# Two-matmul SiLU kernel: the fourth 128-row piece of x and the first columns of w1 change places on one DMA queue, and the first column tiles are cut 384 + 128 rows instead of 256 + 256

## The chip, the cores and the metric

One core of a Trainium2 chip runs the kernel. The time is device microseconds for one launch, as the median of the runs; the profile is one further execution, whose span runs from its first to its last profiled instruction. Engines in the profile: PE is TensorE (matmuls), PEld its weight loads, DVE is VectorE, ACT is ScalarE, POOL is GpSimd, SP is SyncE, which here only issues DMAs. ACT issues some DMAs too ("ACTq").

## The reference

All three inputs are bf16: `x` is 1 x 2048 x 640, `w1` is 640 x 1728, `w2` is 1728 x 640.

```
h   = einsum("bsd,df->bsf", x, w1)      # 2048 x 1728
h   = silu(h)                           # h * sigmoid(h)
out = einsum("bsf,fd->bsd", h, w2)      # 2048 x 640
```

## The kernel before

The kernel is written as a plan: `add(engine, emit, deps)` appends one operation, and `build` emits each engine's operations in the order in which they were added, with a semaphore wait ahead of an operation for each dependency. Nothing is reordered afterwards, so the order of the `add` calls is the order of every engine's queue. An engine that waits holds up all that was added for it later.

The rows of x (2048) are worked in four chunks of 512 rows (`sc` = 0 to 3). The first matmul needs x transposed (`xT_sb`: 128 of the 640 inputs on the partitions, in five groups `dt`, and the rows along the free dimension). Chunks 1 to 3 are transposed by DMA (L230). Chunk 0 would come too late that way: it is loaded plainly in four 128-row pieces j = 0 to 3 (`load_x0`, L144, 160 KB each), and PE transposes each piece in five 128 x 128 steps (L166) into two PSUM banks, 2j and 2j+1. DVE copies three of the five results to `xT_sb` (L172), ACT the other two (L174).

`w1` comes in four DMAs (`load_w1`, L149) of 256, 256, 512 and 704 columns; `w1_0` is the first one, the columns of output tiles `ft` = 0 and 1 (320 KB). Before the change, ACT issues piece 1, piece 3 and then `w1_0`; SP issues pieces 0 and 2 and, when piece 2 has landed, the other three parts of w1, then the transposing DMAs and w2.

While the first loads are under way PE runs six matmuls on constants (L157, five of 512 columns and one of 256), whose results are not used. Then come the 20 transposes, and then the first matmul in units. `unit(sc, ft, c0, n)` is one output tile of 128 columns of w1 by n rows of x: five matmuls that accumulate over `dt` in one PSUM bank (L208), then `silu`: ACT writes the sigmoid to SBUF (L192) and DVE multiplies it with the PSUM tile into `hT_sb` (L195). Unit after unit takes the next of eight banks. A unit of chunk 0 waits for the copies of the last piece that its rows touch, and for its part of w1:

```
def x_deps(sc, c0, n):
    return xT_ready[(c0 + n) // P - 1] if sc == 0 else [x_dma[sc]]
```

The tiles `ft` = 0 and 1 of chunk 0 are cut along the rows at `XE`, which is 256 before the change: two units on rows 0 to 255 (pieces 0 and 1), then two on rows 256 to 511. Every later unit has 512 rows. After 13 full tiles for each chunk and the 64-column tail of w1 (L218), the second matmul (L282) runs to the end, with 64-row weight tiles in pairs; DVE (L294) and ACT (L297) move its results out of PSUM, and SP stores them.

Of the kernel before, what the change touches and what calls it, by code (L numbers as in the profile page):

```python
# [20 lines left out]
class Plan:  # L21
# [9 lines left out]
    def add(self, eng, emit, deps=(), group=None):  # L31
        op = Op(eng, emit, [d for d in deps if d is not None], group)
        self.ops.append(op)
        return op
# [40 lines left out]
def bass_standalone__dense_activation_silu__prompt_kernel(  # L75
# [13 lines left out]
    P = 128  # L89
    H = P // 2  # L90
    SCH = 512
# [6 lines left out]
    JB = SCH // P  # L98
# [4 lines left out]
    with ExitStack() as es:  # L103
        def sb(name, shape, dtype):
            return es.enter_context(nc.sbuf_tensor(name, shape, dtype))
# [8 lines left out]
        x0_sb = sb("x0_sb", [P, JB, D], bf16)  # L114
        ident = sb("ident", [P, P], bf16)
# [9 lines left out]
        bank_free = [[] for _ in range(NBANK)]  # L125
        turn = [0]

        def take_bank():
            b = turn[0] % NBANK
            turn[0] += 1  # L130
            return b


        XE = 2 * P
        w1_cuts = [0, 2, 4, 8, FT]
        id_a = add("pool", lambda e: e.memset(ident[:, :], 0.0))  # L136
        id_b = add("pool", lambda e: e.affine_select(  # L137
            out=ident[:, :], in_=ident[:, :], compare_op=ALU.not_equal, fill=1.0,
            base=0, pattern=[[-1, P]], channel_multiplier=1), [id_a])
# [3 lines left out]
        def load_x0(eng, j):  # L143
            return add(eng, lambda e: e.dma_start(  # L144
                out=x0_sb[:, j, :], in_=x0_v[:, j, :]), group=f"x0_{j}")

        def load_w1(eng, g, deps=()):
            f0, f1 = w1_cuts[g] * P, min(w1_cuts[g + 1] * P, F)
            return add(eng, lambda e: e.dma_start(  # L149
                out=w1_sb[:, :, f0:f1], in_=w1_v[:, :, f0:f1]), deps, group=f"w1_{g}")  # L150

        x0_of = [load_x0(eng, j) for j, eng in enumerate(("sp", "act", "sp", "act"))]
        w1_dma = [load_w1("act", 0)] + [load_w1("sp", g, [x0_of[2]]) for g in (1, 2, 3)]

        ones = nc.const_aps.tensor(1.0, [P, SCH], bf16)
        for n in [SCH] * 5 + [2 * P]:
# [1 line left out]
                ps[:, NBANK - 1, 0:n], lhsT=ones[:, 0:P], rhs=ones[:, 0:n], start=True, stop=True))  # L158

        xT_ready = []  # L160
        for j in range(JB):
            cols = slice(j * P, (j + 1) * P)
            ready = []
            for b, d0, d1, eng in ((2 * j, 0, TPV, "dve"), (2 * j + 1, TPV, DT, "act")):
                for dt in range(d0, d1):
                    t = add("pe", lambda e, j=j, b=b, dt=dt, d0=d0: e.transpose(  # L166
                        ps[:, b, :].bitcast(bf16)[:, (dt - d0) * P:(dt - d0 + 1) * P],
                        x0_sb[:, j, dt * P:(dt + 1) * P], ident[:, :]), [x0_of[j], id_b])
                src = ps[:, b, :].bitcast(bf16)[:, 0:(d1 - d0) * P].rearrange("p (k s) -> p k s", s=P)
                dst = xT_sb[:, d0:d1, cols]  # L170
                if eng == "dve":
                    c = add("dve", lambda e, src=src, dst=dst: e.tensor_copy(out=dst, in_=src), [t])  # L172
                else:
                    c = add("act", lambda e, src=src, dst=dst: e.copy(out=dst, in_=src), [t])  # L174
                ready += [c] * (d1 - d0)
                bank_free[b] = [c]
            xT_ready.append(ready)

        def x_deps(sc, c0, n):
            return xT_ready[(c0 + n) // P - 1] if sc == 0 else [x_dma[sc]]  # L180

        def w1_deps(ft):
            return [w1_dma[max(g for g in range(len(w1_dma)) if w1_cuts[g] <= ft)]]
# [5 lines left out]
        def silu(b, parts, n, pe):  # L189
            s = sig_turn[0] % NSIG  # L190
            sig_turn[0] += 1
            a = add("act", lambda e: e.activation(  # L192
                out=sig_sb[:, s, 0:n], in_=ps[:, b, 0:n], func=ACT.Sigmoid), [pe, sig_free[s]])
            for rows, ft, cols in parts:
                v = add("dve", lambda e, rows=rows, ft=ft, cols=cols: e.tensor_tensor(  # L195
                    out=hT_sb[rows, ft, cols], in0=ps[rows, b, 0:n], in1=sig_sb[rows, s, 0:n],
                    op=ALU.mult), [a])
                chunk_done[cols.start // SCH] = v
                if ft == FR:
                    tail_done[cols.start // SCH] = v  # L200
            bank_free[b] = [v]
            sig_free[s] = v

        def unit(sc, ft, c0, n):
            b = take_bank()
            cols = slice(sc * SCH + c0, sc * SCH + c0 + n)
            for dt in range(DT):
                pe = add("pe", lambda e, dt=dt: e.matmul(  # L208
                    ps[:, b, 0:n], lhsT=w1_sb[:, dt, ft * P:(ft + 1) * P], rhs=xT_sb[:, dt, cols],
                    start=(dt == 0), stop=(dt == DT - 1)),  # L210
                    x_deps(sc, c0, n) + w1_deps(ft) + bank_free[b] if dt == 0 else ())
            silu(b, [(slice(0, P), ft, cols)], n, pe)
# [27 lines left out]
                    w2_dma.append(add("sp", lambda e, hh=hh: e.dma_start(  # L240
                        out=w2_sb[hh * H:(hh + 1) * H, FR, :], in_=w2[FR * P:F, :]), group="w2"))

        for c0 in (0, XE):
            for ft in range(2):
                unit(0, ft, c0, XE)
        for ft in range(2, FR):
            unit(0, ft, 0, SCH)

# [18 lines left out]
        for pi, (sa, sbt) in enumerate(pairs):  # L267
# [3 lines left out]
            for q in range(4):  # L271
                h = q % 2
                c0, c1 = (LAST_SPLIT if pi == len(pairs) - 1 else SPLIT)[h:h + 2]
# [5 lines left out]
                for ft in range(n_ft):  # L279
                    for t, rows in ((lo_t, slice(0, H)), (hi_t, slice(H, P))):  # L280
                        b = banks[t, h]
# [9 lines left out]
                for k, t in enumerate((sa, sbt)):  # L291
                    b = banks[t, h]
# [45 lines left out]
```

## Time and profile before

| | |
|---|---|
| median of 3 runs | 127.2 us (127.02, 127.20, 129.05) |
| the profiled execution, its own time | 127.36 us |
| its span | 125.9 us |
| PE busy | 122.1 us (97% of the span) |
| DVE busy | 48.4 us (38%) |
| ACT busy | 42.4 us (34%) |
| first matmul of the first unit (L208) starts at | 6.03 us |

The profiled execution's time is 1.5 us more than its span: that lies before the first and after the last profiled instruction. "Busy" for PE counts overlapping matmuls once, and a matmul's record is longer than the spacing of matmuls in a stream, as they are pipelined; where a cost per matmul is needed, the spacing of the starts is used. In a timeline line the first number is the start in the span, the second the length, and the bracket holds the idle time before it on that engine and what ended it. A merged line ("x45") covers several instructions in a row.

### The profile page before, as it was taken

The page shows a single profiled execution, that of the slowest core. Times are in us where ns is not written, and L with a number is a line of the kernel's source. Part 1 is how long each engine was busy: PE and PEld are TensorE (multiplying, and loading weights), DVE is VectorE, ACT ScalarE, POOL GpSimd, SP SyncE. Part 2 cuts the span into 40 slices and gives each one's busy share as a digit, 9 for nine tenths or more (in the row PEclk, how much of TensorE's full clock was granted, in tenths as well). Part 3 has the DMA queues.
Part 4 walks back from the last instruction along what each step waited for, and adds up shares of the span by engine and source line. Part 5 has one row for each costly group of instructions (what it writes and reads, how often), then busy time and mean ns, then how long its engine had stood idle before and what let it go on. Part 6 is the DMA issues. An engine that isn't in the chain of part 4 may idle for free.

```text
span 125.9 us, 2647 instructions
## 1 busy us (share of the span) xinstructions
PE 122.1 (97%) x1175; PEld 72.0 (57%) x1180; DVE 48.4 (38%) x79; ACT 42.4 (34%) x78; POOL 0.7 (1%) x6
## 2 busy tenths in 40 slices
PE   7899999999999999999999999999999999999993
PEld 2774444444444444444457777777777777777662
DVE  0454666666666666666673111103011110301103
ACT  4445555555555555555540111102011110201102
POOL 2000000000000000000000000000000000000000
PEclk9999999999999999999999999999999999999999
DMA  4898743599900000000000030200202020020303
GB/s 122 232 346 262 117 84 86 94 346 386 191 7 0 5 0 3 0 0 0 0 5 0 0 109 0 79 31 0 104 5 104 0 85 24 5 104 0 109 0 104
DMA packets 15819, 9.92 MB, mean 79 GB/s; under 512 B 8896, under 2 KB 15808, under 8 KB 15808
## 3 DMA queue, kind: packets, MB, share of 16 engines
q1 hardware_dynamic: 14576, 8.93, 24.5%
q10 hardware_dynamic: 1232, 0.82, 2.1%
q8 instruction: 9, 0.15, 0.5%
q14 instruction: 2, 0.02, 0.0%
HBM read 5.16 MB, written 2.62 MB: 62 GB/s over the span
## 4 chain that ended last, share of the span: by engine, by line
PE 97%; issue 0%; ACT 0%; DVE 0%
PE ps L282 47%; PE ps L208 45%; PE ps L157 2%; PE ps L218 2%; PE ps L166 2%; ACT xT_sb L174 0%; DVE o_sb L294 0%
## 5 line engine op out<-in xcount | busy, mean ns | idle before, releaser
L282 PE MATMUL ps<-w_sb,hT_sb 64*128 64x320 bf16 (+2 forms) x864 | 58.9, 296 | 0.0
L208 PE MATMUL ps<-xT_sb,w_sb 128*128 128x512 bf16 (+1 forms) x265 | 56.3, 373 | 0.8 <-ACT xT_sb L174 0.5
L282 PEld LDWEIGHTS ps<-w_sb,hT_sb 64*128 64x128 bf16 x864 | 41.7, 94 | 17.4 <-issue 0.4
L195 DVE TENSOR_TENSOR hT_sb<-ps,sig_sb 128x512 bf16<-128x512 f32 (+2 forms) x58 | 39.1, 673 | 22.6 <-ACT sig_sb L192 22.2
L208 PEld LDWEIGHTS ps<-xT_sb,w_sb 128*128 128x128 bf16 x270 | 26.5, 98 | 30.4 <-DVE xT_sb L172 0.8
L192 ACT ACTIVATE sig_sb<-ps 128x512 bf16<-128x512 f32 (+1 forms) x56 | 32.6, 582 | 27.1 <-PE ps L208 26.0
L294 DVE CAST o_sb<-ps 128x320 bf16<-128x320 f32 (+2 forms) x16 | 7.9, 491 | 48.9 <-PE ps L282 48.9
L297 ACT CAST o_sb<-ps 128x320 bf16<-128x320 f32 (+2 forms) x16 | 6.8, 425 | 51.7 <-PE ps L282 51.7
L157 PE MATMUL ps<-const-bfloat16-1.0 128*128 128x512 bf16 (+1 forms) x6 | 2.5, 588 | 0.8 <-PEq L323 0.8
L172 DVE COPY xT_sb<-ps 128x384 bf16<-128x384 bf16 x4 | 1.4, 358 | 3.4 <-PE ps L166 3.4
L166 PEld LDWEIGHTS ps<-ident,x_sb 128*128 128x128 bf16 x20 | 2.1, 147 | 0.6 <-DMA x_sb<-in_x_dram 0.6
L218 PE MATMUL ps<-xT_sb,w_sb 128*64 128x512 bf16 x20 | 2.4, 382 | 0.0
L166 PE MATMUL ps<-ident,x_sb 128*128 128x128 bf16 x20 | 2.3, 313 | 0.0
L174 ACT COPY xT_sb<-ps 128x256 bf16<-128x256 bf16 x4 | 1.5, 372 | 2.2 <-PE ps L166 2.2
L157 PEld LDWEIGHTS ps<-const-bfloat16-1.0 128*128 128x128 bf16 x6 | 0.7, 133 | 1.9 <-issue 1.9
L218 PEld LDWEIGHTS ps<-xT_sb,w_sb 128*64 128x64 bf16 x20 | 1.1, 110 | 1.2 <-issue 0.4
L141 ACT ACT_TABLE_LOAD x1 | 1.3, 1283 | 0.7 <-PEq L323 0.7
L140 DVE MEMSET warm_sb<- 128x32 f32 x1 | 0.1, 85 | 0.8 <-PEq L323 0.8
L137 POOL TENSOR_SCALAR_AFFINE_SELECT ident<-ident 128x128 bf16<-128x128 bf16 x1 | 0.3, 292 | 0.2 <-POOL ident L136 0.2
L141 ACT ACTIVATE warm_sb<-warm_sb 128x32 f32<-128x32 f32 x1 | 0.2, 229 | 0.0
L136 POOL MEMSET ident<- 128x128 bf16 x1 | 0.2, 204 | 0.3 <-POOLq L323 0.3
L323 POOL MEMSET const-bfloat16-1.0<- 128x1 bf16 x1 | 0.1, 101 | 0.0
(3 smaller groups left out, 0.3 us busy)
## 6 DMA issues: line engine op xcount, KB each, us to landing
out_dram<-o_sb SPq DMA_DIRECT2D x14, 160.0 KB, 1.9
w_sb<-in_w_dram SPq DMA_DIRECT2D x1, 1120.0 KB, 7.6
w_sb<-in_w_dram SPq DMA_DIRECT2D x1, 960.0 KB, 5.4
w_sb<-in_w_dram SPq DMA_DIRECT2D x1, 880.0 KB, 7.0
w_sb<-in_w_dram SPq DMA_DIRECT2D x1, 640.0 KB, 5.3
x_sb<-in_x_dram SPq DMA_DIRECT2D x2, 160.0 KB, 2.6
x_sb<-in_x_dram ACTq DMA_DIRECT2D x2, 160.0 KB, 2.8
w_sb<-in_w_dram ACTq DMA_DIRECT2D x1, 320.0 KB, 4.1
```

The source lines that it names most:

```text
L141: add("act", lambda e: e.activation(out=warm_sb[:, :], in_=warm_sb[:, :], func=ACT.Sigmoid), [warm])
L157: add("pe", lambda e, n=n: e.matmul(ps[:, NBANK - 1, 0:n], lhsT=ones[:, 0:P], rhs=ones[:, 0:n], start=True, stop=True))
L166: t = add("pe", lambda e, j=j, b=b, dt=dt, d0=d0: e.transpose(ps[:, b, :].bitcast(bf16)[:, (dt - d0) * P:(dt - d0 + 1) * P], x0_sb[:, j, d ...
L172: c = add("dve", lambda e, src=src, dst=dst: e.tensor_copy(out=dst, in_=src), [t])
L174: c = add("act", lambda e, src=src, dst=dst: e.copy(out=dst, in_=src), [t])
L192: a = add("act", lambda e: e.activation(out=sig_sb[:, s, 0:n], in_=ps[:, b, 0:n], func=ACT.Sigmoid), [pe, sig_free[s]])
L195: v = add("dve", lambda e, rows=rows, ft=ft, cols=cols: e.tensor_tensor(out=hT_sb[rows, ft, cols], in0=ps[rows, b, 0:n], in1=sig_sb[rows, ...
L208: pe = add("pe", lambda e, dt=dt: e.matmul(ps[:, b, 0:n], lhsT=w1_sb[:, dt, ft * P:(ft + 1) * P], rhs=xT_sb[:, dt, cols], start=(dt == 0), ...
L218: pe = add("pe", lambda e, dt=dt, hh=hh: e.matmul(ps[hh * H:(hh + 1) * H, b, :], lhsT=w1_sb[:, dt, FR * P:F], rhs=xT_sb[:, dt, (sc + hh) * ...
L282: last[t] = add("pe", lambda e, t=t, rows=rows, b=b, n=n, ft=ft, q=q, cols=cols: e.matmul(ps[:, b, 0:n], lhsT=hT_sb[rows, ft, t * P:(t + 1 ...
L294: ev = add("dve", lambda e, t=t, b=b, n=n, cols=cols: e.tensor_copy(out=o_sb[:, t, cols], in_=ps[:, b, 0:n]), [last[t]])
L297: ev = add("act", lambda e, t=t, b=b, n=n, cols=cols: e.copy(out=o_sb[:, t, cols], in_=ps[:, b, 0:n]), [last[t]])
```

## The change

On ACT's queue, `w1_0` is now issued ahead of piece 3 of x. The row cut `XE` becomes 384. The transposes become a function `transpose_x0(j)`: pieces 0 to 2 are transposed first, then comes the unit of tile 0 on rows 0 to 383, then the transposes of piece 3 with their copies, then the unit of tile 1 on rows 0 to 383, and then the two units on rows 384 to 511. The transposes also name the copies that last read their banks as a dependency; at that point of the plan there is none for the banks in question.

```
-        XE = 2 * P
+        XE = 3 * P
...
-        x0_of = [load_x0(eng, j) for j, eng in enumerate(("sp", "act", "sp", "act"))]
-        w1_dma = [load_w1("act", 0)] + [load_w1("sp", g, [x0_of[2]]) for g in (1, 2, 3)]
+        x0_of = [load_x0("sp", 0), load_x0("act", 1), load_x0("sp", 2)]
+        w1_dma = [load_w1("act", 0)]
+        x0_of.append(load_x0("act", 3))
+        w1_dma += [load_w1("sp", g, [x0_of[2]]) for g in (1, 2, 3)]
...
-        for j in range(JB):
+
+        def transpose_x0(j):
...
-                        x0_sb[:, j, dt * P:(dt + 1) * P], ident[:, :]), [x0_of[j], id_b])
+                        x0_sb[:, j, dt * P:(dt + 1) * P], ident[:, :]), [x0_of[j], id_b] + bank_free[b])
...
-        for c0 in (0, XE):
-            for ft in range(2):
-                unit(0, ft, c0, XE)
+        for j in range(3):
+            transpose_x0(j)
+        unit(0, 0, 0, XE)
+        transpose_x0(3)
+        unit(0, 1, 0, XE)
+        for ft in range(2):
+            unit(0, ft, XE, SCH - XE)
         for ft in range(2, FR):
             unit(0, ft, 0, SCH)
```

## The prediction

> **What bounds the kernel now.** I read the page's first lines, then the chain of waits that ended last, then the timeline of the first 14 us, then the groups by form there, and the DMA issues. The page and the chain:
>
> ```profile
> span 125.9 us, 2647 instructions
> ...
> PE 122.1 (97%) x1175; PEld 72.0 (57%) x1180; DVE 48.4 (38%) x79; ACT 42.4 (34%) x78; POOL 0.7 (1%) x6
> ```
>
> ```profile
> 0.77 2.50 PE ps L157 x6
> 3.27 2.23 PE ps L166 x20
> 5.51 0.02 issue
> 5.53 0.38 ACT xT_sb L174
> 5.91 0.12 issue
> 6.03 3.28 PE ps L208 x23
> 9.31 0.05 issue
> 9.36 10.74 PE ps L208 x49
> ```
>
> PE is the bound. From 6.03 us it runs one stream to the end; its only hole is just before that. So whatever moves the start of the steady stream (tile 2 of chunk 0, the first unit that the change leaves alone) moves the end by as much. The timeline of the start:
>
> ```profile
> 0.93 0.87 ACTq L144 DMA_DIRECT2D x_sb<-in_x_dram  x2
> ...
> 1.83 0.47 ACTq L149 DMA_DIRECT2D w_sb<-in_w_dram  x1
> ...
> 5.00 0.37 ACT L174 COPY xT_sb<-ps 128x256 bf16<-128x256 bf16 x1 [0.16 <-PE ps L166]
> 5.32 0.36 DVE L172 COPY xT_sb<-ps 128x384 bf16<-128x384 bf16 x1 [0.18 <-PE ps L166]
> 5.53 0.37 ACT L174 COPY xT_sb<-ps 128x256 bf16<-128x256 bf16 x1 [0.16 <-PE ps L166]
> ...
> 7.07 0.38 ACT L192 ACTIVATE sig_sb<-ps 128x256 bf16<-128x256 f32 x1 [1.16 <-PE ps L208]
> 7.48 2.06 DVE L195 TENSOR_TENSOR hT_sb<-ps,sig_sb 128x256 bf16<-128x256 f32 x4 [1.80 <-ACT sig_sb L192]
> 7.61 0.38 ACT L192 ACTIVATE sig_sb<-ps 128x256 bf16<-128x256 f32 x1 [0.16 <-PE ps L208]
> ...
> 9.78 0.60 ACT L192 ACTIVATE sig_sb<-ps 128x512 bf16<-128x512 f32 x1 [0.70 <-PE ps L208]
> 10.41 0.69 DVE L195 TENSOR_TENSOR hT_sb<-ps,sig_sb 128x512 bf16<-128x512 f32 x1 [0.87 <-ACT sig_sb L192]
> 10.86 0.60 ACT L192 ACTIVATE sig_sb<-ps 128x512 bf16<-128x512 f32 x1 [0.48 <-PE ps L208]
> ```
>
> A narrower window parts ACT's two loads of x, and the DMA list gives the landing of `w1_0`:
>
> ```profile
> 1.35 0.45 ACTq L144 DMA_DIRECT2D x_sb<-in_x_dram  x1
> ```
>
> ```profile
> w_sb<-in_w_dram ACTq DMA_DIRECT2D x1, 320.0 KB, 4.1
> ```
>
> The chain names ACT's last copy (it ends at 5.90) as what released the first unit at 6.03. The code says otherwise: that unit covers rows 0 to 255 and waits for piece 1's copies, done by 4.84. What it really lacks is `w1_0`, issued at 1.83 and landed 4.1 us later; the trace has its last semaphore step at 5.90. So PE stands still from 5.29 (end of the transposes' stream) to 6.03 for weights.
>
> **Two paces of PE.** The granted clock reads 1.00 throughout, but the spacing of starts does not: the 512-column warm-up matmuls lie 0.427 us apart, the 128-column transposes 0.107, the first 256-column matmuls 0.213. From 6.66 us on it is 0.109 for 256 columns (sigmoids 0.545 apart, five matmuls each) and 0.216 for 512 (1.08 apart). So PE is at half pace until 6.66, and full pace is 0.162 for 384 columns by the line through these two.
>
> **The change, part by part.** Everything is reckoned against the start of tile 2, which the trace has at 8.50.
>
> *1. `w1_0` ahead of piece 3.* Its issue moves from 1.83 to piece 3's slot at 1.35, 0.48 earlier, so it lands at 5.42 and lets PE start at 5.55. The other condition, piece 2's copies, is met at 5.37 (ACT's copy that starts at 5.00), plus 0.13 from release to matmul: 5.50. I take 5.55; the bounds are 5.50 (copies) and 6.03 (no gain, if the traffic rather than the issue decides). Piece 3 goes behind the 320 KB, about where `w1_0` landed, 5.9 to 6.3; it is needed at 6.9, and even 7.5 would be hidden by part 4. SP's queue is not touched; its w1 part for tile 2 lands at 7.79 and the next at 9.67, both ahead of need.
>
> *2. Unit of tile 0, 384 rows.* From 5.55 to 6.66 at half pace (0.320 each) 3.47 of its five matmuls run; the other 1.53 take 0.25. Its stream ends at 6.91. Before, the four matmuls ahead of 6.66 did 0.63 us of half-paced work; now it is 1.11 us. So the 0.48 us gained in start is worth only 0.24 us of full-pace work.
>
> *3. Piece 3's transposes, now behind unit 0.* Before they lay inside the wait for `w1_0` and cost nothing; that cover is gone. Price of a 128-column matmul with its weight load at full pace: no row shows one. Lower bound 0.056 (same line; at half pace 128 columns took exactly the streaming time, 0.107). Upper bound 0.082: the spacing of the last stretch's pairs, two 64-row loads with two 192-column matmuls. I take 0.060, near the streaming end, since the loads hid at half pace. Five: 0.30, to 7.21. Unit of tile 1: 5 x 0.162 = 0.81, to 8.02.
>
> *4. The new wait.* The 128-row units need piece 3's copies, and these are queued behind unit 0's SiLU: on ACT behind its sigmoid, on DVE behind its multiply, which itself waits for the sigmoid. The durations, by form in the first 14 us:
>
> ```profile
> L195 DVE TENSOR_TENSOR hT_sb<-ps,sig_sb 128x512 bf16<-128x512 f32 x4 | 2.8, 692 | 2.0 <-ACT sig_sb L192 2.0
> ...
> L192 ACT ACTIVATE sig_sb<-ps 128x512 bf16<-128x512 f32 x4 | 2.4, 597 | 2.1 <-PE ps L208 2.1
> ...
> L195 DVE TENSOR_TENSOR hT_sb<-ps,sig_sb 128x256 bf16<-128x256 f32 x4 | 1.7, 424 | 2.2 <-ACT sig_sb L192 1.8
> L192 ACT ACTIVATE sig_sb<-ps 128x256 bf16<-128x256 f32 x4 | 1.5, 383 | 1.6 <-PE ps L208 1.6
> ```
>
> For 384 columns I take the middles: sigmoid 0.49, multiply 0.56. From the end of unit 0's stream: 0.20 to the sigmoid (before: stream end 6.86, sigmoid 7.07), 0.49, 0.03 to the multiply, 0.56, 0.03 to the next DVE operation, 0.36 for the copy, 0.15 from its end to PE's next matmul: 1.82. So PE resumes at 6.91 + 1.82 = 8.73, while it is done with unit 1 at 8.02: a stall of 0.71 us that before did not have. ACT's copy is done near 8.0 and decides nothing. Behind the waiting matmul is all of PE's work.
>
> *5. The two 128-row units.* 10 x 0.060 = 0.60 (0.56 to 0.82), so tile 2 starts at 9.33.
>
> Sum: 9.33 - 8.50 = +0.83 us. By parts: earlier start -0.24, transposes uncovered +0.30, stall +0.71, narrow matmuls about +0.05 over the streaming of the same columns. Nothing later is nearer to waiting than before, so PE carries it to the end. The profiled execution would go from 127.36 to 128.2; it lies 0.16 above the median, which would go from 127.2 to 128.0.
>
> The Trainium skill, "TensorE: Matmul & The Clock Gate" (section Back-to-back issue gap), speaks against narrow matmuls: it gives about 81 ns for each weight load and matmul pair at 128 columns. By it part 5 would be 0.81 and the sum 1.04 us (128.2); no row here shows that form at full pace. Its section Part 4: PE-mode transpose says of transposes that they don't count as busy for the clock gate. The trace speaks against it: full pace came at 6.66 after a stretch filled from 3.18 to 5.29 by transposes alone and 0.63 us of matmuls. Were it so, and full pace came some 3.4 us after the first real matmul, at 8.95, the sum would be about 1.2 us (128.4).
>
> **The rivals.**
>
> *A: `w1_0` lands no sooner.* For: x's piece 2 on SP's queue moves in the same stretch, and the 4.1 us to landing are mostly not issue time. Against: piece 3, ahead of it now, lands 1.5 us sooner from the same queue. Then the start is 6.03, unit 0's stream ends at 7.15 (1.97 matmuls at half pace, 3.03 at 0.162), tile 2 starts 2.42 later at 9.57: +1.07, 128.3.
>
> *B: no stall.* If piece 3's copies came in time, the sum is 0.83 - 0.71 = +0.12, 127.3, and with the start at its lower bound and 0.056 per narrow matmul no change at all, 127.2. It decides if the copies run ahead of unit 0's SiLU on DVE. For: the copies' inputs are ready at 7.4, the multiply starts only at 7.63. Against: each engine runs in the order of the plan, and the built order has the multiply ahead of the fourth copy.
>
> *C: full pace comes later, in slower runs by enough to pass 2%.* PE now idles from about 4.75 (15 transposes) to 5.55, 0.80 us against 0.74 before, ahead of the switch. One run of before, 129.05, is 1.69 above the profiled one, as 3.4 us more at half pace would make it. If full pace comes 3.4 us later, at 10.07, all of unit 0, transposes and unit 1 run at half pace to 9.29 (5.55 + 1.60 + 0.53 + 1.60; the stall is covered), the narrow units to 10.2: +1.7, 128.9. From a switch later than 11.7 us on it is over 2%; two such misses (13.5) give tile 2's stream an effective start of 11.9, +3.4, 130.6: slower. For: the margin of 0.06 us is small and the stall near 8.0 adds idle time. Against: before it switched with nearly the same idle time.
>
> **How the numbers follow.** Forecast (start earlier, stall on DVE's order): 0.62, own range 127.6 to 128.5. A: 0.14. B: 0.07. C: 0.15, of which 0.03 passes 2%; some 0.02 is left for what I don't see. The range 127.4 to 128.9 leaves out C's far end, B's low end and part of C's near one. Two per cent of 127.2 is 2.5 us, about what a measurement of this kernel can tell from no change; the forecast is a loss of a third of that. Faster by over 2%: 0.01; within: 0.95; slower: 0.04.
>
> **What would show it.** First L208 matmul at about 5.55 (6.03: A). A hole of about 0.7 us on PE ahead of the 128-column matmuls, ended by DVE's copy at L175 (none: B). On DVE, multiply, then copy, back to back. Spacing 0.056 to 0.082 for the narrow matmuls at full pace. Full-pace spacing from 6.66 on (10 or later: C). Tile 2's stream from about 9.3. The prediction is wrong if tile 2 starts before 8.7 or after 9.9.

## The result, and the profile after

The changed kernel takes 127.69 us (median of 20 runs, 127.19 to 128.86), the kernel before 127.17 us (20 runs, 126.72 to 129.05). The ratio is 1.0048, 95% interval 1.003 to 1.0067: a loss of 0.4 to 0.85 us. The ratio leaves out runs more than 1.5% above the fastest of their kernel, which are three of the 20 before (128.88, 128.94, 129.05) and none of the changed kernel, though four of its runs lie at 128.6 to 128.9. The profiled execution took 128.61 us and is one of these four; that has to be kept in mind in reading it.

The head of the page, then the chain of waits in the first 12 us, for the changed kernel (L211 is the first matmul, L169 the transposes, L175 and L177 the copies on DVE and ACT, L195 and L198 sigmoid and multiply):

```profile
span 127.1 us, 2647 instructions
...
PE 123.3 (97%) x1175; PEld 71.8 (56%) x1180; DVE 48.2 (38%) x79; ACT 42.2 (33%) x78; POOL 0.7 (1%) x6
```

```profile
0.73 2.66 DMA x_sb<-in_x_dram
...
3.44 1.80 PE ps L169 x15
5.24 0.02 issue
5.26 0.38 ACT xT_sb L177
5.64 0.09 issue
5.73 1.76 PE ps L211 x5
7.49 0.53 PE ps L169 x5
8.03 2.60 PE ps L211 x18
```

There is no hole in PE after 5.73, although the forecast had one of 0.7 us. The reason stands in the lengths: five 384-column matmuls take 1.6 us by their starts (0.320 apart) and the five transposes behind them 0.53 (0.107 apart). That is half pace: where PE is at full pace, the same forms lie 0.162 and 0.056 apart. By the starts in the trace the spacing falls to full pace only at about 9.07 us, not at 6.66. In this execution unit 0's SiLU and the copies lie beside slow matmuls:

```profile
7.53 0.49 ACT L195 ACTIVATE sig_sb<-ps 128x384 bf16<-128x384 f32 x1 [1.89 <-PE ps L211]
...
8.05 0.56 DVE L198 TENSOR_TENSOR hT_sb<-ps,sig_sb 128x384 bf16<-128x384 f32 x1 [2.65 <-ACT sig_sb L195]
...
8.53 0.35 DVE L175 COPY xT_sb<-ps 128x384 bf16<-128x384 bf16 x1
```

DVE's copy of piece 3 stands behind the multiply as the plan's order has it, and ends at 8.88; PE is done with unit 1 only at 9.25 and waits for nothing. Tile 2 starts at 9.81 by the trace (8.50 before), +1.31 us, and the profiled executions differ by 128.61 - 127.36 = 1.25. So this profile shows rival C in its first form, not the forecast. Whether the forecast's hole is there in the other executions is the first question for the experiments.

`w1_0` landed 4.0 us after its issue at 1.36, at 5.33 by its last semaphore step. The first unit still began only at 5.73, since piece 0 landed at 3.40 here (3.13 before) and the transposes and copies of pieces 0 to 2 followed from there.

### The profile page after: what moved, and what is told of

The parts are those of the page before. It is cut to its first block, busy times and chain, and to the rows that moved or that the text cites. A ratio compares the mean times of both kernels' runs of the same rounds, so it can differ in the third digit from the quotient of the medians.

```text
span 127.1 us, 2647 instructions
## 1 busy us (share of the span) xinstructions
PE 123.3 (97%) x1175; PEld 71.8 (56%) x1180; DVE 48.2 (38%) x79; ACT 42.2 (33%) x78; POOL 0.7 (1%) x6
## 4 chain that ended last, share of the span: by engine, by line
PE 95%; DMA 2%; issue 0%; ACT 0%; DVE 0%
PE ps L289 46%; PE ps L211 45%; DMA x_sb<-in_x_dram 2%; PE ps L169 2%; PE ps L221 2%; ACT xT_sb L177 0%; DVE o_sb L301 0%
## 5 line engine op out<-in xcount | busy, mean ns | idle before, releaser
L211 PE MATMUL ps<-xT_sb,w_sb 128*128 128x512 bf16 (+2 forms) x265 | 57.6, 377 | 0.8 <-ACT xT_sb L177 0.5
L198 DVE TENSOR_TENSOR hT_sb<-ps,sig_sb 128x512 bf16<-128x512 f32 (+3 forms) x58 | 38.9, 673 | 24.1 <-ACT sig_sb L195 24.0
L211 PEld LDWEIGHTS ps<-xT_sb,w_sb 128*128 128x128 bf16 x270 | 26.3, 99 | 31.2 <-issue 1.0
L195 ACT ACTIVATE sig_sb<-ps 128x512 bf16<-128x512 f32 (+2 forms) x56 | 32.4, 582 | 28.4 <-PE ps L211 27.3
L169 PEld LDWEIGHTS ps<-ident,x_sb 128*128 128x128 bf16 x20 | 2.1, 148 | 1.2 <-DMA x_sb<-in_x_dram 0.9
L175 DVE COPY xT_sb<-ps 128x384 bf16<-128x384 bf16 x4 | 1.4, 356 | 3.4 <-PE ps L169 3.4
L169 PE MATMUL ps<-ident,x_sb 128*128 128x128 bf16 x20 | 2.5, 313 | 0.2 <-DMA x_sb<-in_x_dram 0.2
L177 ACT COPY xT_sb<-ps 128x256 bf16<-128x256 bf16 x4 | 1.5, 373 | 2.3 <-PE ps L169 2.3
```

What stands on the lines that cost most here:

```text
L195: a = add("act", lambda e: e.activation(out=sig_sb[:, s, 0:n], in_=ps[:, b, 0:n], func=ACT.Sigmoid), [pe, sig_free[s]])
L211: pe = add("pe", lambda e, dt=dt: e.matmul(ps[:, b, 0:n], lhsT=w1_sb[:, dt, ft * P:(ft + 1) * P], rhs=xT_sb[:, dt, cols], start=(dt == 0), ...
```

## The experiments

Theory: the loss is PE's wait for DVE's copy of piece 3, queued behind unit 0's multiply, less what the earlier start gives. Rivals: the uncovered transposes and narrow matmuls; a later full pace. Ratios are to runs of the kernel before that were made beside them.

**Copies ahead of the SiLU** (x1). The emission of unit 0's SiLU is held back until piece 3's transposes and copies are in the plan:

```
-        unit(0, 0, 0, XE)
+        held = unit(0, 0, 0, XE, hold=True)   # matmuls only; returns the SiLU
         transpose_x0(3)
+        held()
         unit(0, 1, 0, XE)
```

> The changed kernel, but piece 3's copies stand ahead of unit 0's sigmoid and multiply on ACT and DVE. Theory (the loss is mainly PE waiting for DVE's copy, which is queued behind unit 0's multiply): 0.5 us faster than the changed kernel, so about 127.1, ratio to the kernel before 0.998 to 1.001; no hole on PE ahead of the 128-column units. Rival (the loss is the uncovered transposes, the narrow matmuls and a later full pace): no change against the changed kernel, 127.6 to 127.8, ratio 1.004 to 1.005.

Measured: 126.91 us (12 runs, 126.59 to 128.12), ratio 0.9989 (0.9963 to 1.0014). The loss is gone, as the theory has it. Not all of that need be the copies' place: none of these runs is at 128.5 or above, and PE's work up to the end of unit 1 is that of the changed kernel, which has such runs. The timeline of its profile, an execution at full pace from 4.4 us on:

```profile
5.51 0.97 PE L211 MATMUL ps<-xT_sb,w_sb 128*128 128x384 bf16 x5 [0.69 <-DMA w_sb<-in_w_dram]
...
6.32 0.44 PE L169 MATMUL ps<-ident,x_sb 128*128 128x128 bf16 x5
...
6.60 1.97 PE L211 MATMUL ps<-xT_sb,w_sb 128*128 128x384 bf16 x17
6.69 0.36 DVE L175 COPY xT_sb<-ps 128x384 bf16<-128x384 bf16 x1 [1.59 <-PE ps L169]
```

DVE copies at 6.69, straight behind the transposes, and PE's line from 6.60 on carries no idle bracket. Transposes, narrow matmuls and the new order on the DMA queue are all still in this kernel.

**Tiles alone** (x2): the changed kernel with piece 3 ahead of `w1_0` again.

```
-        x0_of = [load_x0("sp", 0), load_x0("act", 1), load_x0("sp", 2)]
-        w1_dma = [load_w1("act", 0)]
-        x0_of.append(load_x0("act", 3))
-        w1_dma += [load_w1("sp", g, [x0_of[2]]) for g in (1, 2, 3)]
+        x0_of = [load_x0(eng, j) for j, eng in enumerate(("sp", "act", "sp", "act"))]
+        w1_dma = [load_w1("act", 0)] + [load_w1("sp", g, [x0_of[2]]) for g in (1, 2, 3)]
```

> The changed kernel with the old order on ACT's DMA queue (piece 3 ahead of w1's first columns). Theory (the earlier w1 columns are worth 0.24 to 0.48 us): 128.0 to 128.3, ratio 1.007 to 1.009, first unit at about 6.0. Rival (w1's columns do not land sooner in effect, other landings decide): like the changed kernel, 127.6 to 127.8, ratio 1.004 to 1.005.

Measured: 129.02 us (6 runs, 127.64 to 129.38), ratio 1.0114 (1.0069 to 1.016). Slower than the changed kernel, as the theory has it, and by more than it said: four of the six runs lie at 129 and above or just below, the other two at 127.64 and 128.05. These four have the length of the changed kernel's late executions, so most of the 1.1% may be those and not the later `w1_0`; the other two are too few to put a price on that. PE's timeline in the run of 128.05, at full pace from 5.17:

```profile
6.28 0.97 PE L209 MATMUL ps<-xT_sb,w_sb 128*128 128x384 bf16 x5 [1.40 <-DMA w_sb<-in_w_dram]
7.09 0.44 PE L167 MATMUL ps<-ident,x_sb 128*128 128x128 bf16 x5
7.37 0.98 PE L209 MATMUL ps<-xT_sb,w_sb 128*128 128x384 bf16 x5
8.69 0.95 PE L209 MATMUL ps<-xT_sb,w_sb 128*128 128x128 bf16 x11 [0.35 <-DVE xT_sb L173]
```

Here the hole shows, and DVE's copy is named as what ended it. The bracket's 0.35 is counted from the modelled end of the last wide matmul; by starts, 8.018 to 8.691, less 0.162 for its stream, PE loses 0.51 us.

**Queue alone** (x3): the kernel before with the new order on ACT's DMA queue (the reverse of the last diff), nothing else.

> The kernel before with the new order on ACT's DMA queue alone: all 20 transposes still stand ahead of the first unit. Theory (piece 3 now lands where w1's columns did, and its transposes hold up the first unit): first unit at 6.1 to 6.4, 127.3 to 127.5, ratio 1.001 to 1.003. Rival (the earlier w1 columns gain wherever piece 3 lies): 126.7 to 126.9, ratio 0.996 to 0.998.

Measured: 127.44 us (12 runs), ratio 1.0015 (0.9983 to 1.0046). As the theory has it, though the interval holds no change too; the rival's gain (0.998 or less) is all but shut out. The timeline shows the price: piece 3's transposes, which waited for nothing before, wait for a DMA, and the first unit starts at 6.08.

```profile
5.79 0.45 PE L168 MATMUL ps<-ident,x_sb 128*128 128x128 bf16 x5 [0.81 <-DMA x_sb<-in_x_dram]
6.08 2.56 PE L210 MATMUL ps<-xT_sb,w_sb 128*128 128x256 bf16 x21
```

So neither half of the change is good alone: the queue order needs piece 3's transposes moved, and moving them without it leaves PE waiting for w1.

**Even cut with copies first** (x4): x1 with `XE = 2 * P`.

> As the first of these runs, and the row cut back at 256: 256-row units throughout, no narrow matmuls. Theory: first unit at 5.5, piece 3's five transposes between the first two units, copies ahead of the SiLU, stall of 0.1 us at most: 0.1 to 0.3 us faster than the kernel before, 126.9 to 127.1, ratio 0.998 to 0.999. Rival (time of full pace decides, and PE idles longer ahead of it): 127.2 to 127.5, ratio 1.000 to 1.002.

Measured: 127.63 us (12 runs, 126.76 to 129.14), ratio 1.003 (0.9997 to 1.0062). A miss. Its profile starts at 5.13, is at half pace to 6.64 and reaches tile 2 at 8.47, as good as before (8.50); three of its runs lie at 128.66 and above. One of the fill runs below takes this up.

**The same three at full pace.** In place of the first six matmuls on constants there are 35, and all loads of x wait for the 24th, so PE should be at full pace when they land; 16 narrow ones follow the transposes that precede the first unit:

```
+        for _ in range(24):
+            gate = dummy(SCH)
+        for _ in range(11):
+            dummy(SCH)
...
-                out=x0_sb[:, j, :], in_=x0_v[:, j, :]), group=f"x0_{j}")
+                out=x0_sb[:, j, :], in_=x0_v[:, j, :]), [gate], group=f"x0_{j}")
```

> The kernel before, with all of its first loads held back until 24 matmuls on constants are done, 11 more such matmuls during the loads, and 16 narrow ones after the transposes, so that PE has full pace before its first unit whatever the run. It computes the same. About 7 us longer than the kernel before. It is the base for the next two: no number of its own tells theories apart, except that from the first unit on the spacing is 0.109 throughout.

> The changed kernel held back and kept at full pace in the same way. Theory (stall of 0.7 us on DVE's order, transposes 0.28, earlier start worth its full 0.48 at full pace): 0.5 to 0.6 us longer than the kernel before treated in the same way, a hole of 0.7 us on PE ahead of the 128-column units. Rival (the loss came from the later full pace): no hole, and equal within 0.2 us.

> The same with piece 3's copies ahead of unit 0's SiLU. Theory: 0.7 us shorter than the changed kernel at full pace and 0.1 to 0.2 us shorter than the kernel before at full pace; no hole. Rival: equal to the changed kernel at full pace.

Measured, 6 runs each: 134.69, 134.62 and 134.55 us, ratios 1.0558 (1.0516 to 1.0599), 1.0561 (1.0527 to 1.0594), 1.0557 (1.0525 to 1.0589). As times these decide nothing: the instant at which the 24th matmul is done itself depends on when full pace comes (SP issues its first load at 8.91, 8.37 and 9.04 in the three profiles), and that spreads each kernel's runs over a microsecond. The expected differences of 0.5 to 0.7 are not seen in them. The traces, read from that first issue, do decide. From first unit to tile 2 it is 2.18 us before, 2.98 in the changed kernel, 2.46 with the copies first. From the issue to tile 2 it is 7.37, 7.81 and 7.16; the first of these holds some 0.2 us of my own, as the narrow matmuls on constants ran past the landing of `w1_0`. The timeline of the changed kernel at full pace:

```profile
14.21 0.49 ACT L202 ACTIVATE sig_sb<-ps 128x384 bf16<-128x384 f32 x1 [1.40 <-PE ps L218]
...
14.73 0.56 DVE L205 TENSOR_TENSOR hT_sb<-ps,sig_sb 128x384 bf16<-128x384 f32 x1 [2.05 <-ACT sig_sb L202]
15.21 0.35 DVE L182 COPY xT_sb<-ps 128x384 bf16<-128x384 bf16 x1
...
15.61 0.95 PE L218 MATMUL ps<-xT_sb,w_sb 128*128 128x128 bf16 x11 [0.35 <-DVE xT_sb L182]
```

Sigmoid, multiply, copy, PE: the chain of part 4, with the same hole as in x2 (starts at 14.936 and 15.609). With the copies first the hole is not there, as there is no idle bracket on PE behind unit 0, and the two kernels' stretches differ by 2.98 - 2.46 = 0.52, which is the hole. PE in w_copyfirst, then in w_before:

```profile
14.55 0.44 PE L176 MATMUL ps<-ident,x_sb 128*128 128x128 bf16 x5
...
14.83 1.75 PE L218 MATMUL ps<-xT_sb,w_sb 128*128 128x384 bf16 x16
```

```profile
14.10 2.56 PE L218 MATMUL ps<-xT_sb,w_sb 128*128 128x256 bf16 x21
```

**The changed kernel again** (a2).

> The changed kernel once more, for a second profile and more times. Theory (the time when full pace comes differs from execution to execution and decides the rest): if full pace comes before 7 us, a hole of 0.5 to 0.8 us ahead of the 128-column units and 127.2 to 128.0 for that execution; if it comes at 9 us, no hole and 128.5 or more. Rival: no hole in either case. Ratio 1.003 to 1.007.

Measured: 12 runs, median 128.3 (127.25 to 129.37), ratio 1.0054 (1.0022 to 1.0086). The runs fall in two groups, six from 127.25 to 127.92 and six from 128.68 to 129.37. The profiled one (129.21) is of the second: half pace to about 10.07, first unit at 6.00 as `w1_0` landed at 5.86, no hole. That fits the part of the expectation on late executions; the other part it can't show. So both profiles of the changed kernel are of late executions, and the hole itself is seen only in kernels that share its order on DVE (x2, w_after and, below, y3). Of the 17 runs of the kernel before that were made beside these 12, none is at 128 or above.

**Filling PE's idle time.** Six 128-column matmuls on constants behind the transposes that precede the first unit:

```
+        for _ in range(6):
+            add("pe", lambda e: e.matmul(
+                ps[:, NBANK - 1, 0:P], lhsT=ones[:, 0:P], rhs=ones[:, 0:P], start=True, stop=True))
```

(In the kernel before they write bank 0, whose copy is done by then.)

> The changed kernel with piece 3's copies ahead of unit 0's SiLU, and six 128-column matmuls on constants (0.64 us at half pace) where PE waits for w1's first columns. Theory (idle time ahead of the first unit decides whether full pace comes at 4 to 7 us or one step of 3.4 us later; the filling takes the late executions away): all runs between 126.5 and 127.2, median 126.8, ratio 0.996 to 0.998. Rival (late full pace comes by chance whatever PE does): one run in six or so at 127.8 to 128.7, as without the filling.

> The kernel before with the same six matmuls behind its 20 transposes. Theory: no run at 128.3 or above, median 127.0 to 127.2, ratio 0.998 to 1.001. Rival: runs at 128.8 to 129.1 stay, some one in ten.

> The changed kernel with the same six matmuls behind the first 15 transposes; the DVE order, and so the hole of 0.5 us, stays. Theory: no run at 128.3 or above, median 127.4, ratio 1.002 to 1.003. Rival: one run in three at 128.5 to 128.9, as in the changed kernel, median 127.7.

> As the first of these, with the row cut at 256, so with no narrow matmul in a unit. Theory: like the first one within 0.1 us, 126.7 to 126.9, ratio 0.996 to 0.998, no run above 127.5. Rival (the even cut is slower in itself, as its run without filling suggested): 127.2 or more, ratio above 1.000.

| kernel with the filling, 12 runs each | median us | lowest to highest | ratio, 95% interval |
|---|---|---|---|
| y1: copies first | 127.01 | 126.44 to 128.46 | 1.0002 (0.9975 to 1.0029) |
| y2: before | 127.40 | 127.00 to 128.10 | 1.0021 (1.0003 to 1.0039) |
| y3: changed | 127.52 | 127.18 to 128.19 | 1.0038 (1.0019 to 1.0058) |
| y4: even cut, copies first | 127.18 | 126.78 to 127.82 | 1.0006 (0.9987 to 1.0025) |

The late group of the changed kernel is gone: no run at or above 128.5 of 12, where it had 10 of 32 without the filling. y4 loses the runs at 128.66 and above that x4 had. y2 too has none, but the kernel before had only 4 in the 35 runs beside it, so 12 runs can't tell. y1 keeps two, at 128.06 and 128.46, so the filling doesn't explain every long run, or doesn't always fill enough. And x1 had no run at 128.5 or above without any filling, so the share of such runs differs between sets of runs for other reasons too: that filling takes them away is likely, not shown. On its own the filling makes nothing faster than the kernel before: y2 is slightly slower, with `w1_0` at 6.45 in its profile, and y1 and y4 missed the gain that was expected. The copies' place still shows among these four: y3 less y1 is 0.51 us by medians, though the two intervals touch. The chain of y3's profile, one of the early executions of the changed order:

```profile
1.36 4.21 DMA w_sb<-in_w_dram
5.57 0.14 issue
5.71 0.99 PE ps L211 x5
...
6.72 0.50 ACT sig_sb L195
...
7.24 0.56 DVE hT_sb L198
7.80 0.28 DVE xT_sb L175
8.07 0.04 issue
8.12 2.06 PE ps L211 x16
```

Here the hardware's own chain is the one that the prediction wrote down: w1, unit 0, sigmoid, multiply, copy, narrow units. No version beats both kernels clear of the measurement; x1 is nearest (0.9989, with 1 inside its interval).

## Why the prediction was right, and where its sizes were off

The forecast was +0.83 us, the medians moved by 0.52 and the ratio's interval is 0.4 to 0.85. The mechanism was right and named the right instructions. That the median lies inside the forecast's own range is in part luck: the stall was taken 0.20 us too dear, and the earlier start was credited with 0.24 too little for an execution that has full pace early. Without both errors the sum is +0.39, 127.6, the very end of that range; the late executions, which the forecast had left to rival C, brought the median up again. By steps:

*Earlier start.* Forecast: `w1_0` at 5.42, first unit at 5.55. In the eight profiles with the new queue order and no holding back, `w1_0` landed at 4.99 to 5.86, 5.37 on average; in the three with the old order at 5.90, 6.14 and 6.45. So rival A is out on average, though not in every execution: the 5.86 of a2 is hardly sooner than the 5.90 before. The profiled execution itself started at 5.73, held by the copies, the other condition named.

*Half pace to 6.66.* This term failed: the instant was taken from one execution as if it were the kernel's. The profiles have full pace at 3.5 (y4), 4.4 (x1), 5.2 (x2, y2), 6.0 (y1), 6.6 (x4), 9.07 and 10.07 us (the changed kernel). Where it comes early, the 0.48 us of earlier start count in full, not as 0.24.

*Transposes uncovered and narrow matmuls.* Taken at 0.060 each; at full pace they are 0.056 apart in w_after, x1, x2 and y3, the lower bound. The Trainium skill's 81 ns for such a pair ("TensorE: Matmul & The Clock Gate", Back-to-back issue gap) is not seen here.

*The stall.* Forecast 0.71; measured 0.51 in x2, w_after and y3 alike, three times 0.673 between the starts. Two terms of the 1.82 us were too large. DVE's copy does not start 0.03 after the multiply ends but 0.084 before its record ends (in w_after, 15.205 against 14.731 + 0.558). And PE resumes 0.057 after the copy's end (15.552 to 15.609), not 0.15; I had the latter from the release by a DMA, which the new traces show at 0.135 again. Together 0.21, and 1.82 becomes the 1.60 measured. Rival B is out with this: the order held in every trace of a kernel with this order on DVE.

*Sum at full pace.* From first unit to tile 2, 2.98 - 2.18 = +0.80, less 0.48 for the start: +0.32. The runs below 128 us, 15 of the changed kernel and 17 of the one before, have medians 127.52 and 127.13, +0.39; in a2 and the runs beside it they have 127.63 and 127.38, +0.25. The late executions add the rest. The agreement is good to some tenths only, since 0.48 is by how much sooner `w1_0` is issued, not a measured start: the landings above differ by 0.79 on average, and those of w_before and w_after, from the first issue, by only 0.16, so that pair differs by 7.81 - 7.17 = 0.64 from issue to tile 2 (7.17 is 7.37 less the 0.2).

*Rival C.* It is real, though not as often and as dear as to decide. In the changed kernel some third of the runs (10 of 32 at 128.5 or more) are of that kind, 128.5 to 129.4 where the rival's first form gave 128.9; none passes 2% of the median before. That these runs are late executions is seen in the two that were profiled; in a2 tile 2 started at 10.41, past the 9.9 that the prediction had named as a sign of being wrong. The trace's clock record has the full pace last 119.47 us in the profiles of both kernels, from 6.66 and from 9.07. The Trainium skill ("TensorE: Matmul & The Clock Gate", Part 1: The HAM clock gate) says that PE's activity is judged in free-running windows of about 3.4 us; 119.47 is 35 of these by estimate, so the records agree with it. Read so, again an estimate, the window that ended in full pace at 6.66 before held 0.75 us of idle PE, and the windows that failed in the changed kernel, one ahead of 9.07 and 10.07, held 1.0 and 1.25. That a gap of such a size decides is not shown; for it speaks that with the gap filled the late group is gone in y3 and y4, against it that it is not wholly gone in y1. What sets the exact limit stays open. The change does seem to make late executions more frequent: over all the sets of runs, the kernel before has 10 of 101 at 128.5 or more (3 of 20, 3 of 29, 0 of 17, 4 of 35) and the changed kernel 4 of 20 and 6 of 12.

## What to carry to other kernels

When work is moved off one engine's critical order into another's queue, follow the dependent copy to its place in that queue: here, at full pace, the transposes cost PE 0.28 us, and the copy behind a multiply behind a sigmoid cost it another 0.51, which went away when the copy was put first. A time read from one profile is one draw: an instant that differs from execution to execution (here the start of full pace, 3.5 to 10.1 us) has to enter the sum as a range, and a profile of the changed kernel may show a different draw and hide the very wait one looks for. Where a change has two halves that need each other, run each alone: here the tiles alone cost 1.1%, with four of six runs late, and the queue alone gained nothing.

## What the hardware showed that I had not expected

Two DVE operations in a row can overlap in the records: the copy began some 0.08 us before the end of the multiply ahead of it, in w_after (15.205 against 15.289) and in x2 (8.287 against 8.369). The release of PE took 0.057 us from the end of DVE's copy to the next matmul's start (x2, y3, w_after), 0.098 from the end of ACT's copy (the changed kernel, y1), and 0.135 from a DMA's landing. And the landing of one and the same 320 KB load spread over 0.9 us between the eight profiles with the same queue order (4.99 to 5.86; 5.33 and 5.86 in the two of the changed kernel), nearly twice what the change of order moves its issue.
